# Attention products in column parts, transposes of two blocks together, and one input transfer per block

## The chip, the cores and the metric

One core of one Trainium2 chip runs the kernel as one program. The metric is device time in microseconds (us), from one execution after another of the same program; the figure for a kernel is the median of its runs. A profile is one further execution, recorded instruction by instruction. Engines are named as the profile names them: PE (TensorE products), PEld (its weight loads), DVE (VectorE), ACT (ScalarE), POOL (GpSimd) and SP (SyncE, which here only issues transfers).

## What is computed

Two stages follow each other. First comes chunked attention, over 4 batches, 8 heads, 768 rows and 64 columns a head:

```python
for c in range(nc):                       # chunks of 32 rows
    k_full = concat([mem_k, k_ctx])       # 8 memory rows, 16 rows to the left, the chunk, 8 to the right
    scores = scale * q_c @ k_full.T
    a = exp(scores - max); a = a / sum(a)
    out[c] = a @ v_full
```

The result, as 4 x 768 rows of 512, is the input of a mixture of 8 experts. Each row picks an expert (the largest of 8 logits, or the expert of the row before it where a local gate is at least 0.5), and gets

```python
h = maximum(x @ w1[e], 0)                 # 512 -> 1024
out = p[e] * (h @ w2[e])                  # 1024 -> 512
```

All inputs and outputs are fp32.

## The kernel before

**Blocks.** The 3,072 rows are cut into 32 blocks of 96 rows (`QB`), 8 blocks a batch. A block takes the products of 96 query rows with 128 keys (8 memory rows and a band of 120), for 8 heads. The host lays the inputs out so that a block's q is 128 partitions of 384 floats, its k 128 of 512, its v 128 of 520 (64 value columns and a column of ones for each head, so that the sum of the weights comes out of the same product). `load_qk` and `load_v` issue three transfers a block. `LOADS` is 6 buffers; v is loaded four blocks ahead, after the values of a block, and q and k are loaded four blocks ahead of the scores that are being made, which are themselves two blocks ahead.

**Scores** (`scores`, L336). Two heads share the 128 partitions of q and k, so a product has 64 rows of the array, and the two heads of a pair (`u`) work on the upper and the lower half. The weights are the 128 key columns, the moving operand the 96 query columns; the result `s_ps` has keys on partitions. ACT then takes the exponential with a mask as bias, in three pieces of 32 query columns (L348), into `pt`.

**Values** (`values`, L351). For each head the weights are the 96 columns of `pt`, the moving operand the 65 columns of v; the result `o_ps` has query rows on partitions, in two PSUM buffers of four heads each (`o_ps0`, `o_ps1`, one of each). DVE takes the reciprocal of the sums (L357) and multiplies (L358) into the row tile `x`.

**Turning and routing.** `turned` (L362) transposes a block's x on PE into `xt_ps`, and ACT copies it to `xt` (L366). For every half batch (4 blocks, `HALF`) there follow, each some blocks later: `logits` (L368, four 32-column products side by side, ACT copies `lt_ps`), `logits_turned` (L380, `l_ps`, read by DVE), `route_picks` (L397, nine small DVE operations and one exponential), `route_experts` (L416, transposes into `c_ps`, an ACT copy, a DVE scan), `route_ranks` (L430, a DVE scan), `route_places` (L442, first the DVE product of `rank` and `onehot` on 8 partitions, L446), and `route_rows` (L452, transposes of `rank` from 8 partitions into `r_ps`, DVE operations, four indirect writes of rows to `x_dram` by POOL). All these PSUM tiles share the tag `xps`, of which there are two buffers.

**The order.** PE instructions are pinned to the order of the program. The main loop runs over blocks n:

```python
        if n % PAIR == 0:
            for f in first.pop(n, ()):
                f()
            for m in range(n + PAIR, min(n + 2 * PAIR, NB)):
                begun[m] = begin(m)
```

that is, logits and then the scores of the next two blocks; then in every block the values of n, the transposes of block n-1, and the routing pieces that are planned for n (`after`). The other engines' instructions are ordered by a scheduler.

**Experts.** After block 31 the rows are gathered by expert in tiles of 128 and multiplied with w1 and w2 (`h_ps`, `y_ps`). The first five tiles are planned from the first two batches (`plan_early`, at block 22 and 23), and their weights are issued on SP's queue in 512 KB pieces, one a block from block 24 on. What is left of the routing of the last batch stands between the products of the first two expert tiles (`between`). The last wide tiles also use `unit_product`, whose `yu_ps` products use two halves of 64 columns. The function `general` computes everything in another way and runs only where a check on the sums fails.

Of the kernel before, what the change touches and what calls it, by code (L numbers as in the profile page):

```python
# [43 lines left out]
BRANCH = SURE - 4  # L44
RING = 4
LOADS = 6
PLAN = 3 * E + 5
PAIR = 2
FAR = 4096
# [13 lines left out]
@with_exitstack  # L63
def kernel(
    ctx: ExitStack,
    tc: tile.TileContext,
    q: bass.AP,
    k: bass.AP,
    v: bass.AP,
    w_gate: bass.AP,  # L70
    w_local: bass.AP,
    w1: bass.AP,
    w2: bass.AP,
    out: bass.AP,
):
    nc = tc.nc
    keep = ctx.enter_context(tc.tile_pool(name="keep", bufs=1))
    dram = ctx.enter_context(tc.tile_pool(name="dram", bufs=1, space=bass.MemoryType.DRAM))

    x_dram = dram.tile([E * REGION + 1, XW], I32, name="x_dram")  # L80

    ident = keep.tile([P, P], F32, name="ident")
    make_identity(nc, ident)
    kept_i = keep.tile([1, 1], I32, name="kept_i")


    back = keep.tile([QB, 1, E], F32, name="back")
    nc.gpsimd.iota(back, pattern=[[0, 1], [1, E]], base=-E, channel_multiplier=0, allow_small_or_imprecise_dtypes=True)

    everything(tc, q, k, v, w_gate, w_local, w1, w2, x_dram, out, ident, back, kept_i)  # L90


    kept = nc.values_load(kept_i, min_val=0, max_val=NT * H, skip_runtime_bounds_check_because="a count of sums")
    with tc.If(kept < NT * H):
        general(tc, q, k, v, w_gate, w_local, w1, w2, out, ident, back)


@with_exitstack
def general(ctx, tc, q, k, v, w_gate, w_local, w1, w2, out, ident, back):


    nc = tc.nc
# [24 lines left out]
    for b in range(B):  # L127
        lt = one.tile([QB, NQB, E + 1], F32, name="lt")
        for j in range(NQB):
            n = NQB * b + j  # L130
            qt, kt, vt = (one.tile([P, a, w], F32, name=t) for t, a, w in (("qt", HP, QB), ("kt", HP, P), ("vt", H, VW)))
            for t, a in ((qt, q), (kt, k), (vt, v)):
                nc.sync.dma_start(t, a[n])
            x = one.tile([QB, HP, 2, DH], F32, name="x")
            for u in range(2):
                d = slice(DH * u, DH * u + DH)
# [93 lines left out]


@with_exitstack
def everything(ctx, tc, q, k, v, w_gate, w_local, w1, w2, x_dram, out, ident, back, kept_i):

# [21 lines left out]
        nc.tensor.matmul(z_ps, lhsT=zeros[:, 0:P], rhs=zeros[:, 0:D], start=True, stop=True)  # L258
    nc.gpsimd.dma_start(x_dram[0:1], zeros[0:1].bitcast(I32))

    def load_qk(n, queue=nc.sync):
        qt = ld.tile([P, HP, QB], F32, name="qt")
        nc.sync.dma_start(qt, q[n])
        kt = ld.tile([P, HP, P], F32, name="kt")
        queue.dma_start(kt, k[n])
        return qt, kt

    def load_v(n):
        vt = ld.tile([P, H, VW], F32, name="vt")
        nc.sync.dma_start(vt, v[n])  # L270
        return vt


    qks = {n: load_qk(n, nc.scalar) for n in range(2)}
    qks.update({n: load_qk(n) for n in range(2, LOADS - 2)})
    vts = {n: load_v(n) for n in range(LOADS - 2)}


    wg = once.tile([P, DK, QUARTER], F32, name="wg")
# [52 lines left out]
                            base=0, channel_multiplier=-1)  # L332

    def scores(qt, kt, qb):  # L336

        s_ps = sps.tile([P, 2, 512], F32, name="s_ps")
        st = s_ps[:, :, 0:HP * QB].rearrange("p u (a n) -> p u a n", a=HP)
        for a in range(HP):  # L340
            for u in range(2):
                h = slice(DH * u, DH * u + DH)
                nc.tensor.matmul(st[:, u, a], lhsT=kt[h, a], rhs=qt[h, a], start=True, stop=True)
        pt = sp.tile([P, 2, HP, QB], F32, name="pt")
        m = mask_of(qb)
        for g in range(NG):
            c = slice(CHUNK * g, CHUNK * g + CHUNK)
            nc.scalar.activation(pt[:, :, :, c], st[:, :, :, c], ACT.Exp, bias=m[:, g:g + 1], scale=SCALE)  # L348
        return pt

    def values(pt, vt, n, x):  # L351
        for u in range(2):
            o_ps = ops.tile([QB, HP, VW], F32, name="o_ps", tag=f"o_ps{u}")
            for a in range(HP):
                nc.tensor.matmul(o_ps[:, a], lhsT=pt[:, u, a], rhs=vt[:, 2 * a + u], start=True, stop=True)
            rinv = rinvs[:, n, u]
            nc.vector.reciprocal(rinv, o_ps[:, :, DH:VW])  # L357
            nc.vector.tensor_tensor(  # L358
                x[:, 0:D].rearrange("p (a u d) -> p u a d", u=2, d=DH)[:, u], o_ps[:, :, 0:DH],
                rinv.to_broadcast([QB, HP, DH]), op=ALU.mult)  # L360
# [33 lines left out]
    def begin_route():  # L394
        return {n: sm.tile([QB, NQB, w], F32, name=n, bufs=2) for n, w in (("lt", E + 1), ("ex", E))}
# [34 lines left out]
    def route_ranks(r, b, half):  # L430

        of_half = slice(HQ * half, HQ * half + HQ)
        if half == 0:
            r["rank"] = sm.tile([E, S], F32, name="rank")
        onehot, rank = r["onehot"], r["rank"]
        nc.vector.tensor_tensor_scan(rank[:, of_half], onehot[:, of_half], onehot[:, of_half],
                                     r["edge"] if half else base[b], ALU.add, ALU.max)
        if half == 0:
            r["edge"] = sm.tile([E, 1], F32, name="edge")
        nc.vector.tensor_copy(base[b + 1] if half else r["edge"], rank[:, HQ * half + HQ - 1:HQ * half + HQ])  # L440

    def route_places(r, half):  # L442

        onehot, rank = r["onehot"], r["rank"]
        h = slice(HQ * half, HQ * half + HQ)
        nc.vector.tensor_tensor(rank[:, h], rank[:, h], onehot[:, h], op=ALU.mult)  # L446
        tot = r["tot"] = sm.tile([QB, HALF, 1], F32, name="tot")
        nc.vector.tensor_reduce(tot, r["ex"][:, HALF * half:HALF * half + HALF], axis=AX.X, op=ALU.add)
        nc.vector.tensor_scalar(tot, tot, 1e-9, None, ALU.add)
        nc.vector.reciprocal(tot, tot)  # L450

    def route_rows(r, b, half, x):  # L452

        j = HALF * half
        rank, tot, ex = r["rank"], r["tot"], r["ex"][:, j:j + HALF]
        r_ps = xps.tile([QB, HALF, E], F32, name="r_ps", tag="xps")
        for n in range(HALF):
            nc.tensor.transpose(r_ps[:, n], rank[:, QB * (j + n):QB * (j + n) + QB], identity=ident[:E, :E])
        row = sm.tile([QB, HALF], I32, name="row", bufs=2)
        nc.vector.tensor_reduce(row, r_ps, axis=AX.X, op=ALU.max)  # L460
        nc.vector.scalar_tensor_tensor(ex, r_ps, 0.0, ex, ALU.is_gt, ALU.mult)
# [185 lines left out]
    nc.tensor.matmul, nc.tensor.transpose = pinned(matmul), pinned(transpose)  # L647

    def begin(n):
        ahead = n + LOADS - 2  # L650
        if ahead < NB:
            qks[ahead] = load_qk(ahead)
        return scores(*qks.pop(n), n % NQB)

    xs, xts, lts, routes = {}, {}, {}, {}

# [11 lines left out]
        route_rows(routes[b], b, half, xs[b])  # L668


    first, after = {}, {}

    def plan_at(at, step, f, *args):
        at.setdefault(step, []).append(lambda: f(*args))

    for g in range(NB // HALF):
        b, half = divmod(g, 2)
        n = HALF * g + HALF + 2
        plan_at(first, n, half_logits, g)
        plan_at(after, n, half_turned, g)  # L680
        plan_at(after, n + 1, lambda b=b, half=half: route_picks(routes[b], half))
        plan_at(after, n + 2, lambda b=b, half=half: route_experts(routes[b], half))
        plan_at(after, n + 3, lambda b=b, half=half: route_ranks(routes[b], b, half))
        plan_at(after, n + 3, lambda b=b, half=half: route_places(routes[b], half))
        plan_at(after, n + 4, rows, b, half)

    early = {}
# [39 lines left out]
    plan_at(after, n, plan_begun)  # L727
    plan_at(after, n + 1, planned)
    plan_at(after, n + 2, early_gathered)
    plan_at(after, NB - 3, first_turned)  # L730
    for n in range(NB - 8, NB):
        plan_at(after, n, some_pieces, 1)

    begun = {n: begin(n) for n in range(PAIR)}
    for n in range(NB):
        b, j = divmod(n, NQB)
        if n % PAIR == 0:
            for f in first.pop(n, ()):
                f()
            for m in range(n + PAIR, min(n + 2 * PAIR, NB)):  # L740
                begun[m] = begin(m)
        if j == 0:
            xs[b] = xp.tile([P, NQB, XW], F32, name="x")
            nc.gpsimd.tensor_copy(xs[b][0:QB, :, D + 1:XW].bitcast(I32), token[:, n:n + NQB])
            routes[b] = begin_route()
        if j % HALF == 0:
            xts[n // HALF] = sm.tile([P, DK, HALF, QB], F32, name="xt", bufs=2)
        values(begun.pop(n), vts.pop(n), n, xs[b][0:QB, j])
        if n + LOADS - 2 < NB:
            vts[n + LOADS - 2] = load_v(n + LOADS - 2)  # L750
        if n > 0:
            turn(n - 1)
        for f in after.pop(n, ()):
            f()
    some_pieces(len(early["pieces"]))
    flat = rinvs.rearrange("p n u a o -> p (n u a o)")
    ok = sm.tile([P, (NTILE - EARLY) * PLAN], F32, name="scratch")[0:QB, 0:NB * H]
# [114 lines left out]

    pools = (wa, wa, wb)

    after.setdefault(NB, []).insert(0, lambda: turn(NB - 1))
    left = [f for n in range(NB, NB + HALF + 3) for f in first.pop(n, []) + after.pop(n, [])]
    (TURN, EXPERTS_0, RANKS_0, PLACES_0, LOGITS, ROWS_0, TURNED, PICKS, EXPERTS_1, RANKS_1, PLACES_1,
     ROWS_1) = left
    between = {0: {1: [TURN], 3: [LOGITS], 4: [EXPERTS_0], 5: [TURNED], 6: [RANKS_0, PLACES_0, PICKS]},
# [100 lines left out]
```

## Time and profile before

| | |
|---|---|
| median of 3 runs | 530.55 us (528.65 to 539.9) |
| the profiled execution's own time | 500.6 us |
| its span, first to last instruction | 498.5 us |
| mean granted clock of PE in it | 0.994 |
| first expert product (h_ps) starts at | 112.7 us |
| o_ps products: instructions, PE busy, mean | 512, 49.2 us, 249 ns |
| o_ps weight loads | 512, 46.2 us, 165 ns |
| s_ps products | 512, 33.0 us, 279 ns |
| s_ps weight loads | 512, 30.2 us, 189 ns |
| xt_ps copies by ACT (L366) | 32, 15.3 us, 479 ns |
| transfers of v, k, q | 32 each, 260, 256 and 192 KB, 4.7, 4.9 and 4.3 us from issue to landing |

A row of the profile names line, engine and operation, what is written and read, shape and count; then the busy time in us and the mean length of one in ns; then how long the engine stood idle before them. Instructions of PE overlap: the mean length of a product is from its start until its result has come out, while the next ones are already in the array, so the pace is read from start to start, not from the length. All the attention products appear under one line (L644), because a helper issues them; they are told apart by the names of their tiles. The profiled execution is shorter than all three of the runs.

### The profile page before, as it was taken

To read this page: it belongs to the slowest core of one execution; us is meant where nothing else is said; L and a number is where in the kernel's file an instruction comes from. 1 tells how busy PE (TensorE), PEld (TensorE's weight loads), DVE (VectorE), ACT (ScalarE), POOL (GpSimd) and SP (SyncE) were. 2 spreads that over 40 slices of the span, in tenths; PEclk is the share of its full clock that TensorE was granted. 3 is DMA by queue.
4 is the path that set the end of the run, shared out by engine and by line. 5 is a ranking of instruction groups with operands and counts; after the bars stand their busy time and mean duration, and the time that the engine had idled before them with its cause. 6 is when DMAs were issued, how large, how long until landed. Compare 5 with 4: busy or idle time off the path is not lost. (4 is left out here: it accounts for less than half of the span.)

```text
span 498.5 us, 9231 instructions
## 1 busy us (share of the span) xinstructions
PE 485.0 (97%) x3474; PEld 371.5 (75%) x3474; DVE 109.4 (22%) x437; ACT 111.1 (22%) x234; POOL 99.0 (20%) x151
## 2 busy tenths in 40 slices
PE   8999999999999999999999999999999999999993
PEld 5998888888766777766677776667777666958761
DVE  2456677775435000001000000000000000000000
ACT  4555555542111111111111111110111110201110
POOL 3003222433341122110111111001102110031301
PEclk9999999999999999999999999999999999999997
DMA  8987899999999999998999899995169999921101
GB/s 284 384 268 230 280 280 288 313 352 392 409 328 393 410 408 400 350 313 318 336 333 332 318 322 322 331 339 214 39 214 413 373 400 410 393 70 52 45 29 31
DMA packets 49377, 146.01 MB, mean 293 GB/s; under 512 B 7258, under 2 KB 11358, under 8 KB 49312
## 3 DMA queue, kind: packets, MB, share of 16 engines
q1 hardware_dynamic: 42240, 123.38, 68.6%
q0 software_dynamic: 6784, 21.30, 11.7%
q8 instruction: 34, 0.56, 0.5%
q10 hardware_dynamic: 288, 0.52, 0.3%
q14 instruction: 31, 0.25, 0.1%
HBM read 132.57 MB, written 13.00 MB: 292 GB/s over the span
## 5 line engine op out<-in xcount | busy, mean ns | idle before, releaser
L644 PE MATMUL y_ps<-w_sb,ht 128*128 128x512 f32 x224 | 98.5, 593 | 0.0
L644 PEld LDWEIGHTS h_ps<-held_xt,w_sb 128*128 128x128 f32 x704 | 80.5, 192 | 6.6 <-issue 4.9
L644 PE MATMUL h_ps<-held_xt,w_sb 128*128 128x128 f32 x704 | 81.3, 275 | 0.9 <-ACTq _compat.py:109 0.9
L644 PEld LDWEIGHTS y_ps<-w_sb,ht 128*128 128x128 f32 x224 | 41.5, 190 | 46.9 <-issue 46.6
L796 POOL DMA_INDIRECT out_dram<-y,to x24 | 24.2, 1010 | 240.3 <-ACT y L795 213.2
L780 PEld LDWEIGHTS h_ps<-gxt,w_sb 128*128 128x128 f32 x448 | 51.2, 192 | 2.9 <-issue 2.9
L780 PE MATMUL h_ps<-gxt,w_sb 128*128 128x128 f32 x448 | 51.7, 275 | 0.0
L783 ACT ACTIVATE ht<-h_ps 128x512 f32<-128x512 f32 x42 | 25.1, 597 | 118.9 <-PE h_ps L644 78.1
L791 PE MATMUL y_ps<-w_sb,ht 128*128 128x512 f32 x112 | 49.4, 592 | 0.0
L644 PE MATMUL o_ps<-vt,pt 128*96 128x65 f32 x512 | 49.2, 249 | 0.1
L644 PEld LDWEIGHTS o_ps<-vt,pt 128*96 128x96 f32 x512 | 46.2, 165 | 2.2 <-DVE x L358 0.6
L466 POOL DMA_INDIRECT x_dram<-x,row x32 | 29.6, 926 | 73.9 <-DVE x L464 59.0
L710 DVE COPY held_xt<-g_ps 128x512 f32<-128x512 f32 x12 | 8.3, 689 | 137.5 <-PE g_ps L644 123.0
L791 PEld LDWEIGHTS y_ps<-w_sb,ht 128*128 128x128 f32 x112 | 20.7, 190 | 23.0 <-issue 22.2
L644 PEld LDWEIGHTS s_ps<-qt,kt 64*128 64x128 f32 x512 | 30.2, 189 | 6.8 <-issue 4.6
L644 PE MATMUL s_ps<-qt,kt 64*128 64x96 f32 x512 | 33.0, 279 | 0.4 <-ACT pt L348 0.4
L644 PEld LDWEIGHTS h_ps<-x,w_sb 128*128 128x128 f32 x192 | 31.2, 190 | 1.2 <-issue 1.2
L644 PE MATMUL h_ps<-x,w_sb 128*128 128x192 f32 x192 | 31.9, 327 | 0.0
L348 ACT ACTIVATE pt<-s_ps,mask_mid 128x256 f32<-128x256 f32 x72 | 28.1, 482 | 7.1 <-PE s_ps L644 7.0
L710 DVE COPY gxt<-g_ps 128x512 f32<-128x512 f32 x10 | 6.9, 690 | 95.5 <-PE g_ps L707 52.8
L795 ACT ACTIVATE y<-y_ps,x 128x512 f32<-128x512 f32 x12 | 8.3, 688 | 83.1 <-PE y_ps L644 76.4
L358 DVE TENSOR_TENSOR x<-o_ps,rinvs 96x256 f32<-96x256 f32 x64 | 26.3, 418 | 1.2
(207 smaller groups left out, 375.4 us busy)
## 6 DMA issues: line engine op xcount, KB each, us to landing
w_sb<-in_w_dram SPq DMA_DIRECT2D x192, 512.0 KB, 8.9
vt<-in_v_dram SPq DMA_DIRECT2D x32, 260.0 KB, 4.7
kt<-in_k_dram SPq DMA_DIRECT2D x30, 256.0 KB, 4.9
qt<-in_q_dram SPq DMA_DIRECT2D x32, 192.0 KB, 4.3
kt<-in_k_dram ACTq DMA_DIRECT2D x2, 256.0 KB, 3.3
x_dram<-x,row POOLq DMA_INDIRECT x32, 7.2
out_dram<-y,to POOLq DMA_INDIRECT x24, 7.1
x<-x_dram,rows_late POOLq DMA_INDIRECT x11, 7.2
```

The costliest lines, as they stand in the source:

```text
L348: nc.scalar.activation(pt[:, :, :, c], st[:, :, :, c], ACT.Exp, bias=m[:, g:g + 1], scale=SCALE)
L358: nc.vector.tensor_tensor(x[:, 0:D].rearrange("p (a u d) -> p u a d", u=2, d=DH)[:, u], o_ps[:, :, 0:DH], rinv.to_broadcast([QB, HP, DH]), ...
L466: ins = nc.gpsimd.indirect_dma_start(out=x_dram[:, :], out_offset=bass.IndirectOffsetOnAxis(ap=row[:, n:n + 1], axis=0), in_=x[0:QB, j + n ...
L644: return lambda *a, **k: tc.keep_in_program_order(f(*a, **k))
L710: nc.vector.tensor_copy(xt[:, :, 0:P], g_ps)
L780: nc.tensor.matmul(h_ps[:, m], lhsT=w1_sb[:, kk, P * (g + m):P * (g + m) + P], rhs=xt[:, kk, 0:rows], start=(kk == 0), stop=(kk == DK - 1))
L783: nc.scalar.activation(ht[:, g:g + many], h_ps, ACT.Relu)
L791: nc.tensor.matmul(y_ps, lhsT=ht[:, m, 0:P], rhs=w2_sb[:, m], start=(m == 0), stop=(m == FK - 1))
L795: nc.scalar.activation(y, y_ps, ACT.Copy, scale=xs[:, D:D + 1])
L796: return nc.gpsimd.indirect_dma_start(out=out, out_offset=bass.IndirectOffsetOnAxis(ap=to, axis=0), in_=y, in_offset=None, bounds_check=NT ...
```

## The change

- The three inputs q, k and v become one array `qkv`, 1,416 floats a partition and block. `load` brings a block in one transfer, six blocks ahead, after the values of a block. Blocks 0 and 1 come in three pieces.
- `scores` cuts the 128 key columns into two parts of 64, so that a head pair has four products on quarters of the array.
- `values` cuts the 96 columns of `pt` into 64 and 32, with the second part on the array's columns from 64 on.
- The main loop runs over pairs of blocks: scores of the next pair; values of n; then logits, the transposes of blocks n-2 and n-1, and the pieces planned in `after` for n and n+1; then values of n+1, and the pieces planned in `behind` (`route_picks`, `route_ranks`, `route_places`, which have nothing on PE).
- `ranks` is one tile of 128 partitions, zero but for the first 8, and is transposed as 128 rows; its product with `onehot` goes from DVE to POOL.
- `first_turned` stands one block later; the last two blocks' transposes go between the first expert products together.

```diff
+    def block():
+        return ld.tile([P, BW], F32, name="block")
+    def parts(t):
+        q, k, v = t[:, 0:KEYS], t[:, KEYS:VALS], t[:, VALS:BW]
...
+    def load(n):
+        t = block()
+        nc.sync.dma_start(t, qkv[n])
+        return parts(t)
+    blocks = {}
+    for n in range(PAIR):
+        t = block()
+        nc.sync.dma_start(t[:, 0:KEYS], qkv[n, :, 0:KEYS])
+        nc.scalar.dma_start(t[:, KEYS:VALS], qkv[n, :, KEYS:VALS])
+        blocks[n] = t
+    for n in range(PAIR):
+        nc.sync.dma_start(blocks[n][:, VALS:BW], qkv[n, :, VALS:BW])
+        blocks[n] = parts(blocks[n])
+    blocks.update({n: load(n) for n in range(PAIR, LOADS)})
...
+    ranks = once.tile([P, S], F32, name="ranks")
+    nc.gpsimd.memset(ranks, 0.0)
...
     def scores(qt, kt, qb):
         for a in range(HP):
-            for u in range(2):
-                h = slice(DH * u, DH * u + DH)
-                nc.tensor.matmul(st[:, u, a], lhsT=kt[h, a], rhs=qt[h, a], start=True, stop=True)
+            for c in (slice(0, DH), slice(DH, P)):
+                for u in range(2):
+                    h = slice(DH * u, DH * u + DH)
+                    nc.tensor.matmul(st[c, u, a], lhsT=kt[h, a, c], rhs=qt[h, a], start=True, stop=True,
+                                     tile_position=(DH * u, c.start))
...
     def values(pt, vt, n, x):
             for a in range(HP):
-                nc.tensor.matmul(o_ps[:, a], lhsT=pt[:, u, a], rhs=vt[:, 2 * a + u], start=True, stop=True)
+                for c in (slice(0, DH), slice(DH, QB)):
+                    nc.tensor.matmul(o_ps[c, a], lhsT=pt[:, u, a, c], rhs=vt[:, 2 * a + u], start=True, stop=True,
+                                     tile_position=(0, c.start))
...
-        nc.vector.tensor_tensor(rank[:, h], rank[:, h], onehot[:, h], op=ALU.mult)
+        nc.gpsimd.tensor_tensor(rank[:, h], rank[:, h], onehot[:, h], op=ALU.mult)
...
-        r_ps = xps.tile([QB, HALF, E], F32, name="r_ps", tag="xps")
+        r_ps = xps.tile([QB, HALF, P], F32, name="r_ps", tag="xps")
         for n in range(HALF):
-            nc.tensor.transpose(r_ps[:, n], rank[:, QB * (j + n):QB * (j + n) + QB], identity=ident[:E, :E])
+            nc.tensor.transpose(r_ps[:, n], ranks[:, QB * (j + n):QB * (j + n) + QB], identity=ident)
...
+    for n in range(0, NB, PAIR):
+        pair = range(n, n + PAIR)
+        for m in range(n + PAIR, min(n + 2 * PAIR, NB)):
+            begun[m] = begin(m)
+        for m in pair:
...
+            values(begun.pop(m), blocks.pop(m)[2], m, xs[b][0:QB, j])
+            if m + LOADS < NB:
+                blocks[m + LOADS] = load(m + LOADS)
+            if m == n:
+                for f in first.pop(n, ()):
+                    f()
+                for t in range(max(n - 2, 0), n):
+                    turn(t)
+                for t in pair:
+                    for f in after.pop(t, ()):
+                        f()
+            else:
+                for t in pair:
+                    for f in behind.pop(t, ()):
+                        f()
```

## The prediction

> **What bounds the kernel now.** First the page's busy rows and slices, then the windows of the attention stage, then PE's own timeline in one of its periods.
>
> ```profile
> PE 485.0 (97%) x3474; PEld 371.5 (75%) x3474; DVE 109.4 (22%) x437; ACT 111.1 (22%) x234; POOL 99.0 (20%) x151
> ...
> DVE  2456677775435000001000000000000000000000
> ACT  4555555542111111111111111110111110201110
> ```
>
> PE is busy all through; DVE and ACT matter in the first nine slices (0 to 112 us) alone. That is the attention stage, the only one the change touches: the first expert product starts at 112.7 us.
>
> ```profile
> core 0: us, PE busy (x) PEld busy (x) DVE busy (x) ACT busy (x) POOL busy (x), PEclk, DMA share, GB/s
> ...
> 50.00:75.00 25.00, 24.29 (x312) 21.74 (x310) 17.61 (x73) 13.41 (x34) 6.55 (x8) 1.00 0.90 280
> 75.00:100.00 25.00, 24.25 (x300) 21.61 (x297) 18.87 (x86) 14.05 (x35) 8.58 (x10) 1.00 0.93 303
> ```
>
> PE is over 97% busy, DVE 70 to 75%, ACT 55%: PE sets the pace, DVE is next. DMA moves 280 to 303 GB/s, below the 400 of later slices.
>
> ```profile
> 79.20 0.85 PE L644 MATMUL lt_ps<-xt,wg 128*32 128x384 f32 x8
> 79.98 2.03 PE L644 MATMUL s_ps<-qt,kt 64*128 64x96 f32 x32
> 81.94 1.57 PE L644 MATMUL o_ps<-vt,pt 128*96 128x65 f32 x16
> 83.35 0.50 PE L644 MATMUL xt_ps<-ident,x 96*128 96x96 f32 x4
> 83.78 0.35 PE L644 MATMUL r_ps<-ident,rank 8*96 8x8 f32 x4
> 84.42 0.64 PE L644 MATMUL l_ps<-ident,lt_sb 128*96 128x128 f32 x4 [0.29 <-ACT xt L366]
> 84.89 1.50 PE L644 MATMUL o_ps<-vt,pt 128*96 128x65 f32 x16
> ...
> 457.23 7.13 PE L644 MATMUL y_ps<-w_sb,x 128*128 128x512 f32 x16
> 464.30 3.67 PE L644 MATMUL yu_ps<-w_sb,x 128*64 128x256 f32 x32
> ```
>
> Columns: start, length, engine, line, operation, count. Each fp32 product is two instructions (512 for 256 products). Take off the last one's own length (means on the page) and divide. o_ps: (1.50 - 0.25)/15, 0.085 us each. s_ps: (2.03 - 0.27)/31 = 0.057, but the two row halves run side by side: 0.112 a round of two. yu_ps: 0.106, two column halves side by side, 0.212 a round. y_ps 0.43.
>
> So a round costs the larger of two things. **Weights**: 96 columns 85 ns, 128 columns 112: 0.84 ns a column plus 4, so 64 columns give 58 ns. **Stream**: 256 columns 212, 512 columns 429, so 65 give about 57 and 96 give 83 (xt_ps streams 96 in 83). Both attention products are bound by weights.
>
> **Switches.** The last xt_ps starts at 83.60; r_ps, on 8 rows, starts 0.18 later where the cadence is 0.083. s_ps to o_ps takes 0.20; y_ps to yu_ps 0.52 against 0.43. After it the first round is some 0.05 longer. A change of the array's division thus costs 0.15 to 0.17 us.
>
> **What the Trainium skill says.** "TensorEngine Tiling (Array Packing)", Key Properties: changing the tiling mode, not just the tile, drains the engine, and different tiles load and multiply in parallel. The trace agrees with both (0.16 us a switch; yu_ps, lt_ps). Its Available Configurations list 128x64 and 128x32 as different modes; no instruction of before mixes them. "TensorE: Matmul & The Clock Gate", LDWEIGHTS: time goes with columns, not rows; agrees (85 and 112 ns).
>
> **The change part by part**, per period of four blocks (13.42 us before: s_ps starts at 53.19, 66.56 and 79.98).
>
> Scores: eight rounds a block, now of four 64x64 tiles, 58 ns of weights under 83 ns of stream. 32 x (112 - 83) = 0.93 us saved.
>
> Values: 64 rounds, each now a 64-column and a 32-column part. If these run side by side, 58 for 85: 1.73 us saved. This is the unknown; both ends stand under the rivals.
>
> Switches: before, s to o and back twice, plus lt_ps and r_ps. After, values are column-divided, so o to transposes and back as well: eight of 0.16 plus lt_ps to xt_ps. With the old r_ps and lt_ps ones gone the net is about +0.4. That is why transposes of two blocks stand together: else it would be four more.
>
> r_ps: 128-row transposes, 4 x 0.109 for 0.05: +0.2. The 0.3 us wait of l_ps on ACT goes.
>
> What is late next: the transposes' two PSUM buffers (tag xps). Before, values stood between the transposes of two blocks and hid ACT's copy (479 ns, beginning 0.28 after the last transpose starts). I walk the two kinds of loop, from the first score. Scores last 1.5; ACT's six exponentials (1.09 a block) end at 3.4; values run 1.52 to 2.5. *Loop with c_ps*: both transposes are through at 3.3, ACT copies the first from 3.3 to 3.8, so c_ps stands 0.5; values(n+1) start at 4.26, loop end 5.33. *Loop with lt_ps*: lt_ps 2.6 to 3.3, its copy ends 4.04, so the second transpose waits 0.35, r_ps 0.15 and l_ps 0.15; values(n+1) at 5.68, end 6.75. Sum 12.1 against 13.4: **1.3 us a period**. Without buffer waits it would be 10.9.
>
> DVE: 17.6/25 x 13.4 = 9.4 us of work, less 0.55 for the rank product that goes to POOL: 8.9 of 12.1, so not the bound. But the onehot scan (1.0 us) waits for ACT's copy of c_ps, and the evacuation of values(n+1) is queued behind it: o_ps1 comes free at 1.8 us of the next loop, needed at 2.0. Covered by 0.2 us; gone, it costs a few tenths a period.
>
> POOL: L446 at 545 ns on DVE; "GPSIMD Engine Reference", Elementwise, prices such an operation at 1.96 times DVE, so an estimate of 1.07 us. In the loop four us hide it. For the last half it stands behind an output scatter and four row scatters, which end at 137.3, while r_ps started at 137.7: PE waits 0.8 to 1.3 us once.
>
> Loads: 96 issues become about 34, at SP 0.33 each, which nobody waited for; same bytes. But a block is now loaded after its predecessor's values, not q and k earlier: an odd block's load leads its scores by one loop and one block, 5.3 + 0.7 = 6 us, against 4.3 to 4.9 from issue to landing now, and 708 KB at 380 GB/s is 1.9 us of transfer. I cost it at nothing; in the worst pair 0.5 us. The first four blocks stay bound by DMA (384 GB/s to 25 us): no gain there.
>
> Weights: first pieces are issued at 89.6, 23.1 us before the first expert product; after, 19.8. The tightest pieces landed 8.5 us before use (w1 of tile 1 at 121.1, needed at 129.6). 8.5 - 3.3 - 1 (two whole blocks among them) leaves 4 us: hidden.
>
> Sum: seven full periods 9.4, first and last loop 1, less POOL's 0.9: **9.5 us** (estimate). 500.6 (span 498.5 and 2.1 around it) becomes 491.1, a factor 0.981. The median of the runs is 530.55, 6% above the profiled execution, and the page does not show why; I keep the ratio: **520.5**.
>
> **The rivals.**
> *A, as above.* Ends: without buffer waits the period gains 2.5, 16 to 17 us in all; with DVE's and the block's lateness 4. So 514 to 526.
>
> *B, the parts drain (slower).* 64 and 32 columns are different divisions, and each alternation costs a switch. A part then takes stream 57 + drain 94 + its unhidden load, 174 to 200 ns. If both passes of a part stay together, a head has 2 switches, about 490 ns where A has 116; if interleaved as lt_ps is, 4 and 750. Over 256 heads that is 96 to 162 us on A: 587 to 653 profiled, 622 to 692 of median. It decides from 9 ns a part on (1,024 part instructions eat the 9.5 us); from 19 the kernel is 2% slower. For it: the skill's list. Against: c_ps (40 columns, a transpose) follows xt_ps at the plain 0.083 with no drain; lt_ps and yu_ps mix positions freely, though of one size.
>
> *C, no drain, but unequal parts take turns.* A head's pass is 58 + 58 for 85, so 491.1 + 512 x 0.058 = 521, a median of 552. Against: both existing column divisions overlap.
>
> *D, gain turned into waiting* on ACT's copies, DVE's queue or a late block: 498 to 503, a median of 528 to 533. DVE's 75% speaks for it, PE's nearly waitless row against.
>
> **Numbers.** A 0.63 (0.36 faster, 0.27 within 2%, as its centre lies at 1.9%), B 0.18, C 0.10, D 0.09 (0.07 within, 0.02 slower). Faster 0.36, within 2% 0.34, slower 0.30; 2% is about what a measurement of this kernel can tell from no change. A alone is 514 to 526. To leave out no more than B and A's tails the range takes in D and C: 509 to 556.
>
> **What would show it.** s_ps rounds of four at 83 ns; o_ps pairs at 58 ns (A), 116 (C) or 350 and more (B); s_ps starts 12.1 us apart per four blocks; idle time of PE at c_ps and xt_ps put down to ACT xt; PE waiting on POOL at the last r_ps; first h_ps at about 103 us; no wait for w_sb. I am wrong if o_ps pairs aren't near 58, or if score products wait for the block's DMA.

## The result, and the profile after

| | before | after |
|---|---|---|
| median of the runs | 529.6 us (520.9 to 539.9, 4 runs) | 597.0 us (591.0 to 602.4, 4 runs) |
| ratio, with its 95% interval | | 1.134 (1.109 to 1.159): slower |
| profiled execution, its span | 500.6, 498.5 us | 591.0, 589.2 us |
| first expert product starts at | 112.7 us | 202.6 us |
| from there to the end | 385.7 us | 386.6 us |

Ratios, here and below, leave out runs more than 1.5% slower than the fastest of the same kernel, so they are not always the quotient of two medians.

The attention stage is 90 us longer, and nothing else has changed. Summed over the starts of PE's products up to the first expert product, values (o_ps) go from 44.2 to 126.4 us, scores from 32.4 to 34.9, transposes from 13.2 to 17.1. So 82 of the 90 us are the values.

The page after, busy times and slices (columns as before):

```profile
PE 567.5 (96%) x4498; PEld 407.2 (69%) x4498; DVE 106.9 (18%) x429; ACT 110.3 (19%) x234; POOL 107.6 (18%) x160
...
DVE  2223333334333334600000000000000000000000
...
L665 PE MATMUL o_ps<-block,pt 128*64 128x65 f32 (+1 forms) x1024 | 129.1, 241 | 0.7 <-DVE x L379 0.7
```

PE's share is as high as before, and the row of o_ps shows hardly any waiting (0.7 us), but 129.1 us busy for 49.2. A pause between two products, at a change of the array's division, doesn't look like a wait on this page; it hides in busy time. DVE's digits fell from 7 to 3: it has less to do in the same time, since PE feeds it more slowly. The windows of the attention stage, which are to be held against those of before:

```profile
core 0: us, PE busy (x) PEld busy (x) DVE busy (x) ACT busy (x) POOL busy (x), PEclk, DMA share, GB/s
50.00:75.00 25.00, 24.55 (x308) 16.96 (x306) 9.12 (x41) 7.74 (x20) 3.48 (x4) 1.00 0.40 129
75.00:100.00 25.00, 23.45 (x294) 16.13 (x292) 8.59 (x36) 7.51 (x19) 4.81 (x6) 1.00 0.47 150
```

PE gets through about 300 instructions in 25 us as before, though scores and values now have twice as many of them; DMA moves half (129 to 150 GB/s for 280 to 303). PE's timeline in one loop:

```profile
83.83 3.88 PE L665 MATMUL o_ps<-block,pt 128*64 128x65 f32 x31
87.64 1.55 PE L665 MATMUL s_ps<-block 64*64 64x96 f32 x64
89.12 3.94 PE L665 MATMUL o_ps<-block,pt 128*64 128x65 f32 x31
```

The score group is as the prediction has it: 1.55 less the last product's own 0.25, 64 instructions in rounds of four, 83 ns a round. The value group is not: a block's values last 3.9 us, where they lasted 1.50 to 1.57 before, in half as many instructions. One head inside such a group, starts of its four products (us):

```
84.208  64 columns, first pass
84.316  64 columns, second pass    108 ns after
84.467  32 columns, first pass     151 ns
84.549  32 columns, second pass     82 ns
84.699  next head                  150 ns
```

At every change of size, in both directions, the next product starts 150 ns later, and the one after it is late too (108 and 82 ns; in e3 below, products of one size follow each other after 56 to 60). That makes 490 ns a head, where a head was 171 before.

### The profile page after: what moved, and what is told of

It is laid out like the page before. It is cut to its first block, busy times and chain, and to the rows that moved or that the text cites. A ratio compares the mean times of both kernels' runs of the same rounds, so it can differ in the third digit from the quotient of the medians.

```text
span 589.2 us, 11150 instructions
## 1 busy us (share of the span) xinstructions
PE 567.5 (96%) x4498; PEld 407.2 (69%) x4498; DVE 106.9 (18%) x429; ACT 110.3 (19%) x234; POOL 107.6 (18%) x160
## 5 line engine op out<-in xcount | busy, mean ns | idle before, releaser
L665 PE MATMUL o_ps<-block,pt 128*64 128x65 f32 (+1 forms) x1024 | 129.1, 241 | 0.7 <-DVE x L379 0.7
L665 PEld LDWEIGHTS o_ps<-block,pt 128*64 128x64 f32 (+1 forms) x1024 | 84.8, 122 | 44.0 <-issue 2.1
L665 PE MATMUL s_ps<-block 64*64 64x96 f32 x1024 | 28.4, 247 | 7.5 <-issue 5.1
L665 PEld LDWEIGHTS s_ps<-block 64*64 64x64 f32 x1024 | 23.6, 133 | 11.8 <-issue 8.8
L378 DVE RECIPROCAL rinvs<-o_ps 96x4 f32<-96x4 f32 x64 | 11.4, 179 | 108.1 <-PE o_ps L665 101.7
L465 POOL TENSOR_TENSOR ranks<-ranks,onehot 8x384 f32<-8x384 f32 x8 | 7.9, 984 | 119.5 <-DVE edge L459 78.2
```

The source lines that it names most:

```text
L465: nc.gpsimd.tensor_tensor(rank[:, h], rank[:, h], onehot[:, h], op=ALU.mult)
L665: return lambda *a, **k: tc.keep_in_program_order(f(*a, **k))
```

## The experiments

In all of them the time from the first expert product to the end stays at 386 to 391 us, so the time of that product ("first h_ps") tells the rest. Experiments e1 to e4 ran on a chip where the kernel before took 499.9 us (498.8 to 500.3, 7 runs); e5 to e12 and e13 to e18 ran on two others, where its medians were 530 to 536. Ratios compare runs on one chip. The expectations of e1 to e4 give spans, which are some 2 us shorter than times; their "theory D" is the drain, which the prediction has as rival B.

**The sizes of the parts (e1 to e4, e8).** Four edits of the changed kernel, each in `values`, and one of the kernel before:

```diff
 e1: values whole, as before the change
+                nc.tensor.matmul(o_ps[:, a], lhsT=pt[:, u, a], rhs=vt[:, 2 * a + u], start=True, stop=True)
 e2: 64 and 64 columns (pt laid flat; the second part reads 32 columns too many)
-                for c in (slice(0, DH), slice(DH, QB)):
+                at = QB * (HP * u + a)
+                for c in (0, DH):
+                    nc.tensor.matmul(o_ps[c:c + DH, a], lhsT=pt[:, at + c:at + c + DH], rhs=vt[:, 2 * a + u],
+                                     start=True, stop=True, tile_position=(0, c))
 e3: all heads' 64 columns, then all heads' 32
+            for c in (slice(0, DH), slice(DH, QB)):
+                for a in range(HP):
 e4: three parts of 32
+                for c in (slice(0, 32), slice(32, 64), slice(64, QB)):
 e8: the kernel before, with the values of the changed kernel and nothing else of it
+                for c in (slice(0, DH), slice(DH, QB)):
```

Expected of e1: 

> The changed kernel with the values' products whole again (96 columns, one instruction pair a head), all else kept. Theory D (each change between a 64-column and a 32-column part drains the array): o_ps goes from 490 ns a head back to 170, 256 heads, so 82 us less, and the two extra switches a pair of blocks (16 x 2 x 0.16 = 5 us) go too: span near 502 us from 589. Rival R1 (column parts of one head take turns whatever their sizes) and rival R2 (1,024 more instruction pairs starve PE of instructions) expect the same here; they part in the next two kernels. If the paired transposes or the block's one transfer were to blame, the span would stay above 560.

Expected of e2: 

> The changed kernel with both parts 64 columns wide: the second part takes columns 64 to 127 of a head, of which the last 32 are the next head's and are not used. Same number of instructions as the changed kernel, more work in them. Theory D: no change of size is left, a pair of parts costs one round of 58 ns, a head 116 ns instead of 490: 256 x 0.374 = 96 us less, span near 493 us. R1 (parts of one head take turns): a pass costs 116, a head 232: span near 523. R2 (number of instructions): no change, near 589.

Expected of e3: 

> The changed kernel with the same instructions in another order: in each o_ps buffer first the 64-column parts of four heads, then their 32-column parts. Theory D: 2 changes of size per buffer instead of 8. A buffer costs 8 x 58 + 8 x 57 + 2 x 0.16 us = 1.24 instead of 1.96 us, 64 buffers: 46 us less, span near 543. R2 (number of instructions) and R1: no change, near 589.

Expected of e4: 

> The changed kernel with three equal parts of 32 columns: 512 more instruction pairs than the changed kernel has. Theory D: three parts of one size side by side, a pass is bound by the stream of 65 columns, 57 ns, a head about 116: span near 493 as with two equal parts, plus what a stretch of missing instructions costs (the changed kernel shows PE standing some 1.7 us in every second group of scores without a named release). R1: three parts in turn, 3 x 57 a pass, 342 a head: span near 551. R2: worse than the changed kernel, above 600.

Expected of e8: 

> The kernel before with only the values' product in parts of 64 and 32 columns. Theory (the two sizes are different divisions of the array and each alternation drains it): a head costs 490 ns where it cost 171, so 256 heads add 80 to 85 us: 580 to 585 us, whatever the loop's order. Rival (the drain appears only together with the change's other parts, its order or its waits): under 550 us.

| | time us | ratio to before (interval) | first h_ps us |
|---|---|---|---|
| e1 | 511.5 | 1.024 (1.022 to 1.025) | 122.1 |
| e2 | 511.0 | 1.024 (1.019 to 1.028) | 120.6 |
| e3, one run | 535.1 | | 146.3 |
| e4 | 522.5 | 1.044 (1.041 to 1.047) | 135.8 |
| e8, one run | 620.3 | | 232.5 |

The values of one block in e2, e4, e3 and e8, in this order:

```profile
95.02 1.15 PE L672 MATMUL o_ps<-block,pt 128*64 128x65 f32 x32
65.13 1.11 PE L665 MATMUL o_ps<-block,pt 128*32 128x65 f32 x48
71.07 2.43 PE L665 MATMUL o_ps<-block,pt 128*64 128x65 f32 x32
67.60 3.99 PE L646 MATMUL o_ps<-vt,pt 128*64 128x65 f32 x32
```

The mixture of sizes is the cause. Parts of 64 and 64 run side by side: from first to last start 32 instructions take 0.93 us, 60 ns a round, which is about the rate that the forecast took for 64 and 32. Three parts of 32 do as well, 48 instructions in 0.89 us. With the sizes apart (e3), eight switches in a group of four heads become two, the block takes 2.21 us for 3.77, and the first h_ps comes 56 us earlier than in the changed kernel (46 were expected). And in the kernel before with the mixed parts alone (e8), the block takes 3.77 us from first to last start where the clock is full, as in the changed kernel: no other part of the change is needed for it.

e8 as a whole took 620 us and not the 580 to 585 expected. Its windows from 50 to 72 us and from 75 to 100 us (columns as above):

```profile
50.00:72.00 22.00, 22.00 (x217) 15.67 (x216) 7.84 (x32) 7.22 (x18) 0.00 (x0) 1.00 0.43 131
75.00:100.00 25.00, 25.00 (x146) 16.48 (x145) 6.22 (x25) 4.55 (x11) 2.44 (x3) 0.50 0.34 99
```

The granted clock of PE is half for 88.8 us before the first expert product (72.6 to 140.9 and 178.5 to 198.9 us), against 6.8 us in the changed kernel, and a block's values take 5.87 us in these stretches. So the 89 us between e8 and the kernel before on its chip (531.3) are not the price of the mixture alone; that price is read at the full clock. What brought the half clock there stays open: since 10 us PE had not stood longer than 0.3 us.

e1, e2 and e4 were expected at spans of 502, 493 and about 493 and have 508.6, 507.3 and 522.5; e1 and e2 are 11 us above the kernel before. In e4 PE stands 15 us with no named release in the waits of o_ps and s_ps, and 27 us before the first expert product are at half clock. In e1 and e2 part of the loss is one wait. PE's timeline in e2:

```profile
97.61 0.55 PE L672 MATMUL xt_ps<-ident,x 96*128 96x96 f32 x4 [0.17 <-ACT lt_sb L405]
104.56 1.09 PE L672 MATMUL r_ps<-ident,ranks 128*96 128x128 f32 x4 [6.39 <-POOL ranks L472]
105.44 1.06 PE L672 MATMUL l_ps<-ident,lt_sb 128*96 128x128 f32 x4
106.43 1.90 PE L672 MATMUL o_ps<-block,pt 128*64 128x65 f32 x32
```

and POOL's in the same stretch:

```profile
97.48 0.99 POOL L631 DMA_INDIRECT xs<-x_dram,rows_early  x1 [7.62 <-DVE x L386]
...
102.55 0.95 POOL L631 DMA_INDIRECT xs<-x_dram,rows_early  x1 [0.30 <-issue]
103.52 0.98 POOL L472 TENSOR_TENSOR ranks<-ranks,onehot 8x384 f32<-8x384 f32 x1
```

The rank product, moved to POOL, takes 0.98 us as estimated, but stands behind the five early gathers (the three left out lie between). PE stands 6.4 us, and then works at half pace: the same 32 products take 1.90 for 1.15, r_ps 1.09 for 0.61. The Trainium skill, "TensorE: Matmul & The Clock Gate", What's actually happening, says that the array runs at half its clock after an idle stretch of some 3.4 us. Here the trace agrees: the clock is recorded at half from 101.3 us, 3.1 us into the wait, to 108.1.

**The parts one by one, and where their gain went (e5 to e7, e10, e11).**

```diff
 e5: e2, with
-        nc.gpsimd.tensor_tensor(rank[:, h], rank[:, h], onehot[:, h], op=ALU.mult)
+        nc.vector.tensor_tensor(rank[:, h], rank[:, h], onehot[:, h], op=ALU.mult)
 e6: the kernel before, with the changed kernel's scores
 e7: e6, with e2's values
 e10: e5, with the scores of the kernel before
 e11: the kernel before, with e2's values
```

Expected of e5: 

> The kernel of e2 (the change with 64 and 64 columns a values pass) with the rank product back on VectorE, all else of the change kept. In e2 PE once stood 7.0 us before r_ps, released by POOL's product, which was queued behind the early gathers, and then ran some 10 us at a lower clock. Theory: that one wait and the clock after it are what kept e2 slower than the kernel before. Then the long r_ps wait goes, and the first expert product starts at 110 us or earlier (e2: 120.6); the time is 0.98 to 1.00 of the kernel before. Rival: the paired transposes, the buffer waits and the stalls within the scores are to blame: it stays at 1.015 to 1.025, first expert product at 118 or later. Second rival: POOL's queue delays the gathers' own consumers too: a wait of some us stays at another place near 97 us.

Expected of e6: 

> The kernel before with only the scores changed: four 64x64 products a head pair, nothing else of the change. Theory (a round costs its stream, 83 ns for 112): 32 rounds in a period of 13.4 us save 0.9, seven to eight periods 7 us, so 0.985 of the kernel before, period 12.5 us. Rival: the scores' 512 more instructions make PE stand within the score groups for no semaphore (in the changed kernel every second loop's group took 3.0 us for 1.3): then the gain is 0 to 2 us, ratio 0.995 to 1.00, and issue shows before s_ps.

Expected of e7: 

> The kernel before in its own order (transposes after each block, separate loads, rank product on VectorE) with scores in four 64x64 tiles and values in two parts of 64 columns (the second part's last 32 columns are not used). Theory: values save 1.7 us a period, scores 0.9, and four to eight switches more at 0.16 take 0.7 to 1.3 back: period about 12.0 us for 13.4, in all 9 to 11 us, ratio 0.98; it comes out at or ahead of e5. Rival (instruction supply): 1,024 more instructions in 100 us, PE stands with issue: ratio 0.99 to 1.01.

Expected of e10: 

> The kernel of e5 with the scores as before (two 64x128 products a head pair): of the change there remain one DMA a block, the paired transposes and values in two parts, here of 64 and 64 columns; the rank product is on VectorE. Theory (a score group of four tiles is what PE's supply doesn't keep up with beside the row scatters): fewer and shorter gaps than in e5, ratio 0.975 to 0.995. Rival (the paired transposes and the single DMA cost the time): 1.01 to 1.02 as in e5.

Expected of e11: 

> The kernel before with only the values in two parts of 64 columns (the second part's last 32 columns are not used). Theory: 1.7 us a period saved, six to eight switches of 0.15 more, so 0.6 us a period and 4 to 6 us in all, ratio 0.985 to 0.995. Rival: gaps beside the row scatters grow with the number of instructions: 1.00 to 1.01.

| | time us | ratio to before (interval) | first h_ps us |
|---|---|---|---|
| e5 | 537.0 | 1.020 (1.011 to 1.030) | 145.7 |
| e6 | 536.9 | 1.017 (1.010 to 1.024) | 146.3 |
| e7 | 528.5 | 0.998 (0.995 to 1.000) | 139.2 |
| e10 | 532.2 | 1.006 (0.998 to 1.013) | 139.8 |
| e11 | 529.7 | 0.999 (0.993 to 1.005) | 138.8 |

In e5 the long wait before r_ps is gone, as expected, and yet the time isn't better; but e5 ran on another chip than e2, so what that wait alone cost isn't settled. None of the five brings what its cadences promise: e5, e7 and e11 come out at the ratio of their rival or next to it, e10 lies between theory and rival, and e6 is slower than even its rival allowed. The timeline of e6 shows why:

```profile
44.47 0.96 PE L646 MATMUL s_ps<-qt,kt 64*64 64x96 f32 x32
45.83 0.36 PE L646 MATMUL s_ps<-qt,kt 64*64 64x96 f32 x3 [0.40 <-issue]
47.24 0.31 PE L646 MATMUL s_ps<-qt,kt 64*64 64x96 f32 x2 [1.05 <-issue]
48.66 0.89 PE L646 MATMUL s_ps<-qt,kt 64*64 64x96 f32 x27 [1.11 <-issue]
49.48 2.53 PE L646 MATMUL o_ps<-vt,pt 128*96 128x65 f32 x16
```

A group of 1.5 us takes 5.0, and PE waits for no semaphore ("issue"): two or three products come, then none for a microsecond. Afterwards the values go at half pace, 2.53 for 1.57 (the clock is recorded at half from 49.8 to 60.1 us). It happens once in every four blocks.

**Does the kernel before have it too? (e9)** The same kernel, no edit.

Expected: 

> The kernel before once more, unchanged, for a second profile of it. The first one had a span of 498.5 us and no gap over 0.7 us between the products of the attention stage, while most other runs of the same kernel took about 530. Theory: what is missing are gaps in PE's product stream beside the row scatters, and a lower clock after them, as e5 to e7 show them: at about 530 us the first expert product starts near 140 us, and groups of products that lie in the time of the scatters take 1 to 4 us longer than the same groups elsewhere. Rival: the clock alone is lower (every product longer by the same factor, no gaps). At about 500 us the run tells nothing new.

It took 532.3 us in its one run, with the first h_ps at 141.9. PE's timeline in a loop whose o_ps group took 1.57 us in the first profile too:

```profile
44.89 2.03 PE L644 MATMUL s_ps<-qt,kt 64*128 64x96 f32 x32
46.85 0.47 PE L644 MATMUL o_ps<-vt,pt 128*96 128x65 f32 x3
47.69 0.31 PE L644 MATMUL o_ps<-vt,pt 128*96 128x65 f32 x2 [0.37 <-issue]
49.12 1.87 PE L644 MATMUL o_ps<-vt,pt 128*96 128x65 f32 x11 [1.12 <-issue]
50.78 0.84 PE L644 MATMUL xt_ps<-ident,x 96*128 96x96 f32 x4
```

So the 6% between the profiled execution and the runs of before are such gaps and stretches at half pace: a period of four blocks is 19.7 us here (s_ps starts at 44.89 and 64.56) and 13.4 in the first profile. In e6 the gaps lie in scores, here in values; what is common is the time, 45 to 49 us, in which the four row scatters of a half batch move. Of the 29 us by which the first expert product comes later, 8 are standing (PE's stands of more than 0.15 us add up to 11.8 us for 3.7); by subtraction some 21 lie in the 47.8 us that are recorded at half clock.

**Moving the scatters (e12, e13, e16).** All three are e6 with the scatters held back by two blocks.

```diff
 e12: the scatters of route_rows in a function of their own, planned two blocks later
+            after.setdefault(NQB * b + HALF * half + HALF + 8, []).insert(
+                0, lambda: row_scatters(row, b, half, xs[b]))
 e13: the same, with the row numbers copied there first
+            nc.vector.tensor_copy(late[:, ns[0]:ns[-1] + 1], row[:, ns[0]:ns[-1] + 1])
 e16: in place of the copy (copied is the later block)
+            nc.vector.scalar_tensor_tensor(late[:, c], rinvs[:, copied, 1, c, 0], 0.0, row[:, c], ALU.mult, ALU.add)
```

Expected of e12: 

> The kernel of e6 (scores in four tiles alone) with the row scatters issued two blocks later than their r_ps, all else in place. In e6 the score group that follows r_ps and l_ps took 3.7 to 4.8 us for the 1.3 of an undisturbed one, once a period, always while a half's scatters were moving. Theory (the scatters' traffic starves PE of instructions): the gaps move with the scatters, to the products some 6 us later (the second block's values, lt_ps, or the next score group), and the score group after l_ps takes 1.3 to 2.4 us. Rival (something at that place in the program, such as the loads' landing or a fetch of instructions there): the gaps stay in the group after l_ps.

Expected of e13: 

> The kernel of e6 (scores in four tiles alone) with each half's four row scatters issued behind a copy of their rows on VectorE that stands two blocks later in its queue, so that they can't run ahead of PE. In e6 and e12 they moved within 5 us of r_ps, beside the score group after l_ps (4.8 us for 1.3). Theory (the scatters' traffic makes the gaps): that score group takes 1.3 to 1.5 us and the gaps come 6 us later, beside the second block's values, lt_ps or the next score group. Rival (the place in the program makes them): the score group after l_ps keeps its 3.5 to 5 us.

Expected of e16: 

> The kernel of e6 (scores in four tiles alone), each half's row scatters held until the values of the second block after r_ps are in: their row numbers get those values' reciprocals times zero added. Theory (the scatters' traffic makes the gaps): the score group after l_ps takes 1.3 to 1.5 us (e6, e13: 4.8 to 5.3) and gaps of 2 to 4 us in all come later, beside the transposes, lt_ps, the other score group or the values after it. Rival (the place in the program makes them): the score group after l_ps keeps its 3.5 to 5 us. Time about that of e6, 530 to 537.

Each has one run. e12 (535.6 us) and e13 (533.7) decide nothing: POOL had nothing else to do, and e13's copy was placed right behind its source in DVE's order, so the scatters moved at 45 to 51 us as ever. In e16 (523.9) they depend on a later block's values. POOL and PE there:

```profile
47.60 0.99 POOL L478 DMA_INDIRECT x_dram<-x,late  x1 [41.91 <-DVE late L475]
```

```profile
43.52 1.55 PE L656 MATMUL s_ps<-qt,kt 64*64 64x96 f32 x64
45.00 1.57 PE L656 MATMUL o_ps<-vt,pt 128*96 128x65 f32 x16
...
49.79 1.03 PE L656 MATMUL s_ps<-qt,kt 64*64 64x96 f32 x33
51.20 0.40 PE L656 MATMUL s_ps<-qt,kt 64*64 64x96 f32 x4 [0.37 <-issue]
51.94 0.38 PE L656 MATMUL s_ps<-qt,kt 64*64 64x96 f32 x4 [0.35 <-issue]
```

The scatters start 4.6 us later (42.97 in e6), the score group after l_ps is whole, and the gaps stand in the next one. In this run they follow the scatters, not the place in the program.

The scatters alone don't make gaps, though. In the first profile of before the same four are issued as closely (44.94, 46.24, 47.47 and 48.70 us), and no gap follows. A difference in the DMA packets: those of a half batch's scatters take 7.1 to 8.9 us there and 4.9 to 5.7 in e9. Whether that is a cause or a consequence was not tried, and e8 has no gap at 4.6 us, with products that come far more slowly.

**Spreading them (e14, e15, e17, e18).** One scatter a block in place of four in a row: e14 (kernel before) and e15 (e7) behind a plain copy, which spreads them in part (in e14 three still go together, at 43.9, 45.2 and 46.5 us, and the fourth at 50.8); e18 (kernel before) and e17 (e7) tied to the values as in e16.

```diff
+        for ns, step in (((0,), 0), ((1,), 1), ((2,), 2), ((3,), 3)):
...
+                after.setdefault(step, []).insert(0, lambda ns=ns, step=step: row_scatters(row, b, half, xs[b], ns, step))
```

Expected of e14: 

> The kernel before with a half's four row scatters spread over four blocks, three of them behind a copy of their rows on VectorE. Theory (gaps come from the burst of four scatters, 790 KB in some 5 us, beside the loads): the gaps and the half clock after them go or shrink, ratio 0.95 to 0.98 where the kernel before takes 530, 1.00 where it takes 500. Rival (each scatter makes its gap, 0.6 to 0.7 us, wherever it is): the same sum of gaps in four places, ratio 0.99 to 1.01. Second rival: the copies delay VectorE's queue: 1.00 to 1.01.

Expected of e15: 

> The kernel of e7 (both products in parts, 64 and 64 columns a values pass, in the order of the kernel before) with the same spread scatters. Theory (burst): the gaps of 4.5 us in one score group a period go, period near 12 us, ratio 0.93 to 0.97 where the kernel before takes 530, 0.98 where it takes 500, and 8 to 10 us below e14. Rival (each scatter makes its own gap): ratio 0.99 to 1.00 as e7.

Expected of e17: 

> The kernel of e7 (both products in parts, 64 and 64 columns) with a half's four row scatters one by one, the first at once and each next one held by the values of one block more. Theory (the burst of scatters makes the gaps): no gap over 0.7 us in most periods, period 12 to 13.5 us, ratio 0.95 to 0.98, below e15's 0.985. Rival (each scatter makes its own gap wherever it lies, or held rows delay the early gathers): 0.985 to 1.00.

Expected of e18: 

> The kernel before with its row scatters held and spread in the same way. Theory (burst): gaps and half clock go, period near 13.5 us, ratio 0.955 to 0.98 where the kernel before takes 530, and e17 lies 6 to 10 us below it. Rival (each scatter its own gap): 0.99 to 1.00, as e14.

| | time us | ratio to before (interval) | first h_ps us |
|---|---|---|---|
| e14 | 524.5 | 0.998 (0.993 to 1.003) | not given |
| e15 | 519.9 | 0.985 (0.980 to 0.989) | 133.0 |
| e17 | 509.9 | 0.955 (0.946 to 0.964) | 123.4 |
| e18 | 511.6 | 0.959 (0.951 to 0.968) | 121.1 |

e14's profiled execution took 533.5 us, 9 above its median, so its start isn't given. e14 and e15 miss the 0.95 to 0.98 and 0.93 to 0.97 of their theory. With the tie and the spreading the theory's ratios come (e16, tied but not spread, keeps its gaps): all runs of e17 (512.1 us at most) and e18 (513.2) are faster than the fastest of 28 runs of the kernel before on that chip (520.5). They are not faster than the 500 us of its first profile and of the first chip, where the tie was not tried. In e18 the attention stage is free of gaps up to the early gathers, with the period of the first profile again (44.87 to 58.29):

```profile
44.87 2.03 PE L654 MATMUL s_ps<-qt,kt 64*128 64x96 f32 x32
46.83 1.57 PE L654 MATMUL o_ps<-vt,pt 128*96 128x65 f32 x16
...
51.62 2.03 PE L654 MATMUL s_ps<-qt,kt 64*128 64x96 f32 x32
...
58.29 1.92 PE L654 MATMUL s_ps<-qt,kt 64*128 64x96 f32 x30
```

What it still lacks to 112.7 us is mostly one wait of PE at the early gathers, behind which the held rows seem to queue, and 10 us at half clock from 106.9 us (the waits of e18 from 100 to 114 us: engine and line, what was waited for, us in all, times, the longest; "remote" is a release that the profile can't name):

```profile
DVE rinvs L357 <- remote: 8.9, 1, 8.9
POOL xs L613 <- DMA x_dram<-x,late: 6.9, 1, 6.9
PEld o_ps L654 <- remote: 6.3, 1, 6.3
```

A version that spreads only the scatters before and after the gathers was not tried. e17 was expected 6 to 10 us below e18 and isn't: the intervals overlap. It has the faster products (a group of values 1.15 for 1.57), but gaps stay (6 of them in the scores, 4.5 us in all), and its own waits at the gathers. e15, which has equal parts too, lies 1.3% below e14, and there the intervals don't overlap. So the gain of equal parts is between nothing (e7, e11, e17) and about 1% in these runs.

## Why the prediction was wrong

**The step that failed** is the term of the values: "64 rounds, each now a 64-column and a 32-column part. If these run side by side, 58 for 85". It is the one the prediction called the unknown, and it took the wrong end. They don't run side by side: two switches a head make it 490 ns for the 116 forecast, 82 us more for the values than before where 14 less were forecast, and in e8 the same rhythm stands without any other edit. Rival B named this number ("a head has 2 switches, about 490 ns") and the profiled time it leads to, 587 us; 591.0 was measured. That the sum fits so well is luck in part: the scores came out 2.5 us longer instead of 7 shorter, since five of their groups hold stands, and the rest of the stage, by subtraction, 5 us longer where the forecast's terms make some 12. The evidence that was held against it, c_ps with 40 columns following xt_ps at the plain cadence, was perhaps of another kind: the kernel names no part of the array for that product, and does for the 32-column part. No run tests that. "lt_ps and yu_ps mix positions freely, though of one size" was the better clue, and the half-sentence at its end was the answer. The Trainium skill's "TensorEngine Tiling (Array Packing)", Key Properties, was right as it stood: a change of mode, not of tile, drains. e2 and e4 change the tile alone and pay nothing.

**From the profiled time to the median.** "the page does not show why; I keep the ratio" put 6% on top. In the kernel before those 6% are gaps beside the row scatters and half clock (e9, e16, e18). The ratio doesn't carry over: in the changed kernel gaps add some 1.7 us to each of five score groups between 60 and 180 us, the clock is full up to 190 us, and the median lies 1% over the profiled execution. So B's median of 622 was too high where its profiled time was right.

**POOL's rank product.** The length was right (0.98 us for 1.07), the place not. "In the loop four us hide it" looked at the free time of POOL, not at its queue: the five gathers ahead of it cost 6.4 us in e2 and 7.1 in e1. The changed kernel itself doesn't show this wait; its drains cover it. The prediction priced the queue for the last half only.

**What held.** Score rounds of four at 83 ns, wherever undisturbed. Buffer waits after paired transposes: c_ps 0.48 to 0.54 us (0.5 forecast), the second transpose after lt_ps 0.35 to 0.40 (0.35). Switches of 0.15 to 0.18. No wait for weights; the single transfer of a block costs PE only two waits in all, 2.3 us together. Rounds of two equal parts take 58 to 60 ns (e2), as forecast for the unequal ones. A period of four blocks in e2 is 12.2 to 12.5 us where no gap stands in its scores (12.1 forecast), and 13.0 to 13.6 from there to 77 us, with gaps of 0.9 to 1.4 us in some groups.

**Rival D**, a gain turned to waiting, is what e5, e6, e7, e10 and e11 are like, but by none of its three mechanisms: not ACT's copies, not DVE, not a late block, but gaps in PE's own stream and half clock.

What stays open is how the scatters hold PE back, and what sets the half clock. The Trainium skill, "Runtime: NRT & Kernel Launch", Instruction fetch mechanics, says that instructions stream to the engine in 16 KB blocks and that this is mostly hidden. The gaps look like a supply that runs dry, yet in e9 no 16 KB transfer lies between 45 and 55 us, where the gaps stand at 47 and 48. Nor is it known why one chip (or one execution) shows them and another doesn't.

## What to carry to other kernels

Give parts that share the array one size, as far as these runs tell (64 with 64, three of 32): read the cost of one switch off the trace, count the alternations, and price them before hoping for overlap. When an operation moves to another engine, look for what is queued ahead of it there, not for that engine's idle share. And when runs and profile of a kernel differ by more than the effect in question, take a second profile first: here the difference held more time than the whole change was meant to save.

## What was not expected of the hardware

Between column parts of 64 and 32 the next product starts 150 ns later instead of 58, in both directions, while three of 32 or two of 64 cost nothing. On two of the experiments' three chips, while four indirect row writes issued within 5 us move, PE's products come in twos and threes with 0.6 to 1.4 us from one start to the next; spread one a block, the writes leave e18's stream whole up to the gathers, but not e17's. After two stands of only 0.37 and 1.12 us in e9 PE ran at half pace for 10 us, 160 ns between products for 85; the idle stretch of 3.4 us cited above is longer. In e8 half pace began with no such stand and held for 68 us.
